# Sort matrices turned by a VectorE block transpose, four more heads expanded on GpSimd, and a newly searched order

## The chip, the cores and the metric

One core of a Trainium2 chip. The time is the device time of one execution in microseconds (us); a kernel's time is the median of its executions. The profile's span is shorter than that time by 1.7 to 2.8 us and is used only for readings inside a run. Engines: TensorE (PE, with its weight loads PEld), VectorE (DVE), ScalarE (ACT), GpSimd (POOL), and SP, which issues the transfers.

A run is called slow when it lies over 1.5 % above the fastest of its kernel, and fast otherwise; the granted TensorE clock is read beside it. Every ratio below is the mean time of one kernel's fast runs over that of the other's in the same rounds, with a 95 % interval, so it is not quite the ratio of the medians that stand next to it.

## The reference, cut to what matters

```python
for _ in range(5):                          # sort_net [4, 8, 8, 8]: 32 (batch, head) pairs
    P = exp(P - max(P, -1)); P /= sum(P, -1) + 1e-9; P /= sum(P, -2) + 1e-9
k_sorted = einsum('bhij,bhjcd->bhicd', P, k_b)      # 8 blocks of 96 rows
v_sorted = einsum('bhij,bhjcd->bhicd', P, v_b)
attn     = softmax(scale * q_b @ k_sorted_b.T)      # inside each block
x        = (attn @ v_sorted_b) as [batch, 768, 512]
val, gate = split(x @ w_in)
h[t]     = exp(A_log)[0] * h[t-1] + val[t]          # scan over 768 steps
out      = (silu(gate) * h) @ w_out
```

## The kernel before

The program lists some 250 operations with dependences; a scheduler inside the kernel sorts them into one list per engine before anything is emitted. Before any block can be sorted, the 32 normalised 8x8 matrices (tile PBF, 32 pairs x 64) have to be turned to 64 x 32, spread over the partitions by TensorE, and multiplied by a mask into block-diagonal weights (tile LALL).

```python
op("ptr_mm", PE,  matmul(PS[u.bank][0:64, 0:NH], PBF, IDENT[0:NH, 0:NH]))
op("ptr_cp", DVE, tensor_copy(PT, PS[u.bank][0:64, 0:NH]))
# pexp_mm: 8 x matmul(..., ESEL[:, i * 128:(i + 1) * 128], PT)
# lmat on VectorE, from PSUM: heads 0-1 (256 columns), heads 2-7 (768 columns)
# pexp_cp: ScalarE copies PSUM to PEXP; lmat on GpSimd, from PEXP: heads 8-31, four at a time
...
for it in range(5):                         # warming matmuls, between the rounds of the normalisation
    for part in range(WARMS[it]):
        op("warm", PE, 4 if it < 4 else 8 matmuls of IDENT by IDENT)
...
P.schedule(8, pull=5.859375, stick=0.1, nudge=NUDGE)
```

Names in the views: L609/L554 transposes of q (line before/line after the change), L625/L570 sorted k and v, L703/L648 scores, L733/L678 attention by values, L662/L607 the other sorted values, L776/L721 transposed activations, L800/L745 input projection, L836/L781 output projection, L754 and L751/L699 and L696 normalisation on VectorE/ScalarE, L713/L658 exponentials. VSS to VA are the moves of sorted values, XN to XT the transposes done by DMA. A q behind an engine's name means its sequencer, which issues; "issue" is time in which an engine waited for nothing that the profile shows.

The softmax here doesn't subtract the row's maximum and nothing guards it: scores larger than these inputs give would overflow.

## Time and profile before

| | before |
|---|---|
| median (range) | 124.22 us (123.44 to 124.76), later rounds 123.8 to 124.7 |
| span of the profiled run, granted clock | 121.7 us, 1.00 |
| TensorE busy, idle | 112.2 us, 9.5 us |
| first expansion on VectorE / first projection | 12.3 / 27.5 us |
| batch 1's moved values landed | 40.3 us |

The table is read from below: the work of TensorE is fixed, so the time is that work plus the time in which TensorE stands still.

### The profile page before, as it was taken

Reading aid. Unit: us, or ns where it says so; the run is one execution under the profiler, and the core shown is the slowest. Engines: PE = TensorE matmul, PEld = TensorE weight load, DVE = VectorE, ACT = ScalarE, POOL = GpSimd, SP = SyncE. Lnnn points to the kernel's source line nnn. Section 1 sums busy time; section 2 is a strip of 40 time slices with the busy share of each in tenths; the row PEclk is TensorE's granted clock in tenths of the full one; section 3 lists DMA queues with packets and bytes.
Section 4 is the critical chain, followed back from the end, with each engine's and each line's share of the span. In section 5 each row is a group of like instructions: output and inputs, shape, how many; then the busy total and the mean of one; then the engine's idle time right before and its main releaser. Section 6 shows DMA issues by size and latency. Waiting matters only on the chain.

```text
span 121.7 us, 3684 instructions
## 1 busy us (share of the span) xinstructions
PE 112.2 (92%) x1485; PEld 74.7 (61%) x1485; DVE 100.0 (82%) x239; ACT 84.0 (69%) x183; POOL 59.5 (49%) x84
## 2 busy tenths in 40 slices
PE   1689989999999999999999999999799999999990
PEld 1577778765766777667556586766466655554530
DVE  3774897999998999977599999999799999995300
ACT  4126879999868988898866977887634423365761
POOL 7999999999955620200028065000011396235500
PEclk9999999999999999999999999999999999999999
DMA  1999999999999999999999868289892000422665
GB/s 6 149 176 188 199 212 209 204 205 203 217 247 236 202 208 215 225 251 239 253 293 251 128 102 154 100 151 144 287 260 48 5 0 0 172 89 86 226 252 216
DMA packets 26305, 21.33 MB, mean 175 GB/s; under 512 B 7472, under 2 KB 22832, under 8 KB 26288
## 3 DMA queue, kind: packets, MB, share of 16 engines
q0 software_dynamic: 13824, 11.01, 58.3%
q1 hardware_dynamic: 12464, 10.08, 30.8%
q8 instruction: 12, 0.20, 0.6%
q14 instruction: 5, 0.04, 0.1%
HBM read 22.03 MB, written 6.29 MB: 233 GB/s over the span
## 4 chain that ended last, share of the span: by engine, by line
PE 66%; DMA 10%; DVE 9%; ACT 4%; SPq 4%; POOL 2%; issue 1%; POOLq 0%
PE PSA L800 31%; PE PSA L836 14%; DMA VA<-VSS 6%; PE PSA L733 5%; DVE XN L754 5%; DMA QB<-in_q_dram 4%; SPq L671 4%; PE PSA L703 4%; PE PSA L609 4%; PE PSA L625 3%; PE PSA L662 2%; ACT EX L713 2%; PE PSA L776 1%; DVE XT L417 1%; DVE RZ L745 1%
## 5 line engine op out<-in xcount | busy, mean ns | idle before, releaser
L819 POOL TENSOR_TENSOR GA<-GA,YS 128x384 bf16<-128x384 bf16 x30 | 27.2, 917 | 55.3 <-DVE GA L816 32.0
L800 PE MATMUL PSA<-XT,WIN 128*128 128x384 bf16 x256 | 45.4, 326 | 0.8 <-DVE XN L754 0.8
L800 PEld LDWEIGHTS PSA<-XT,WIN 128*128 128x128 bf16 x256 | 23.9, 98 | 16.3 <-DVE XN L754 0.9
L713 ACT ACTIVATE EX<-PSA 96x384 bf16<-96x384 f32 x64 | 26.3, 488 | 2.4 <-PE PSA L703 2.1
L813 ACT ACTIVATE TH<-PSA 128x384 f32<-128x384 f32 x32 | 15.7, 492 | 15.0 <-PE PSA L800 13.8
L836 PE MATMUL PSA<-WOUT,GA 128*128 128x512 bf16 (+1 forms) x100 | 23.2, 370 | 0.0
L754 DVE TENSOR_TENSOR XN<-PSA,RZ 96x320 bf16<-96x320 f32 (+2 forms) x49 | 21.7, 470 | 0.2
L816 DVE SCALAR_TENSOR_TENSOR GA<-TH,PSA 128x384 bf16<-128x384 f32 x32 | 17.0, 542 | 5.3 <-ACT TH L813 4.2
L415 ACT ACTIVATE OUTSB<-PSA 128x512 f32<-128x512 f32 (+1 forms) x23 | 13.4, 581 | 7.3 <-PE PSA L836 7.1
L807 DVE TENSOR_TENSOR_SCAN YS<-AEXP,YS,PSA 128x384 bf16<-128x384 f32 x16 | 15.7, 999 | 0.3 <-PE PSA L800 0.2
L807 DVE TENSOR_TENSOR_SCAN YS<-AEXP,PSA 128x384 bf16<-128x384 f32 x16 | 14.8, 940 | 0.7 <-PE PSA L800 0.7
L733 PE MATMUL PSA<-VA,EX 96*128 96x65 bf16 x256 | 13.7, 194 | 0.5 <-DVE XN L754 0.2
L836 PEld LDWEIGHTS PSA<-WOUT,GA 128*128 128x128 bf16 x100 | 9.0, 97 | 8.2 <-ACT OUTSB L415 0.3
L733 PEld LDWEIGHTS PSA<-VA,EX 96*128 96x128 bf16 x256 | 10.9, 98 | 4.7 <-DMA VA<-VSS 0.8
L745 DVE RECIPROCAL RZ<-PSA 96x5 f32<-96x5 f32 (+2 forms) x52 | 8.3, 175 | 2.0 <-PE PSA L733 1.6
L415 ACT ACTIVATE KTS<-PSA 128x768 bf16<-128x768 f32 x11 | 8.6, 811 | 1.4 <-PE PSA L625 1.3
L703 PE MATMUL PSA<-QTS,KTS 64*96 64x96 bf16 x256 | 9.5, 210 | 0.0
L703 PEld LDWEIGHTS PSA<-QTS,KTS 64*96 64x96 bf16 x256 | 7.2, 121 | 3.6 <-DVE KTS L417 0.4
L609 PE MATMUL PSA<-IDENT,QB 128*64 128x128 bf16 x192 | 7.8, 238 | 1.3 <-DMA QB<-in_q_dram 1.3
L415 ACT ACTIVATE VSS<-PSA 128x384 bf16<-128x384 f32 x19 | 8.4, 504 | 0.3 <-PE PSA L662 0.3
L625 PE MATMUL PSA<-LALL,KB 128*64 128x128 bf16 x192 | 7.4, 221 | 0.7 <-ACT EX L713 0.6
L427 POOL DMA_DIRECT2D QB<-in_q_dram x10 | 7.7, 782 | 0.3 <-issue 0.3
(60 smaller groups left out, 122.2 us busy)
## 6 DMA issues: line engine op xcount, KB each, us to landing
out_dram<-OUTSB SPq DMA_DIRECT2D x23, 256.0 KB, 2.5
VA<-VSS SPq DMA_DIRECT2D x24, 97.5 KB, 5.7
VB<-in_v_dram POOLq DMA_DIRECT2D x6, 384.0 KB, 20.1
KB<-in_k_dram POOLq DMA_DIRECT2D x6, 384.0 KB, 23.9
QB<-in_q_dram POOLq DMA_DIRECT2D x6, 384.0 KB, 21.5
WIN<-in_moe_w_in_dram POOLq DMA_DIRECT2D x1, 1024.0 KB, 11.1
QB<-in_q_dram POOLq DMA_DIRECT2D x4, 192.0 KB, 5.1
KB<-in_k_dram POOLq DMA_DIRECT2D x4, 192.0 KB, 6.1
```

What stands on the lines that cost most here:

```text
L415: return eng.activation(dst, src, AF.Copy, scale=1.0 if scale is None else scale)
L609: ins = e.transpose(PSB[u.bank][64 * x:64 * x + 64, t * 128:(t + 1) * 128], QB[sl][:, 2 * pr + x, t * 64:(t + 1) * 64], IDENT[:, :])
L703: ins = e.matmul(PS[us[half, x].bank][0:BLK, il * BLK:(il + 1) * BLK], KTS[ks][r, i * BLK:(i + 1) * BLK], qt(r, i))
L713: op("ex%d_%d_%d" % (p, half, x), act_cost(HALF), lambda e, n, u=us[half, x], es=es, half=half: e.activation(EX[es][:, half, 0:HALF].rearr ...
L733: ins = e.matmul(PS[u.bank][:, (kk - k0) * 65:(kk - k0 + 1) * 65], EX[es][:, i // 4, (i % 4) * BLK:(i % 4) * BLK + 128], VA[vs][:, i, hx * ...
L754: return e.tensor_tensor(XN[xs][:, k0 * D:(k0 + nb) * D].rearrange("p (n d) -> p n d", d=D), pv(u, nb)[:, :, 0:64], bass.AP(RZ[rz], 0, [[6 ...
L800: ins = e.matmul(PS[u.bank][:, 0:HALF], WIN[:, c, col:col + 128], XT[(4 * b + c) % NXT][:, half * HALF:(half + 1) * HALF], start=(c == 0), ...
L807: op("sc%d_%d_%d" % (b, ch, half), {"DVE": 65 + 384 * 2.1}, lambda e, n, u=u: e.tensor_tensor_scan(YS[slot][:, :], AEXP[:, ch:ch + 1].to_b ...
L813: op("th%d_%d_%d" % (b, ch, half), act_cost(HALF), lambda e, n, u=w: e.activation(TH[ts][:, :], PS[u.bank][:, 0:HALF], AF.Tanh, scale=0.5) ...
L816: op("ga%d_%d_%d" % (b, ch, half), dve_cost(HALF), lambda e, n, u=w: e.scalar_tensor_tensor(GA[slot][:, :], TH[ts][:, :], 1.0, PS[u.bank][ ...
L819: op("um%d_%d_%d" % (b, ch, half), {"POOL": 900, "DVE": 500} if b == B - 1 and half else {"POOL": 900}, lambda e, n: e.tensor_tensor(GA[sl ...
L836: ins = e.matmul(PS[u.bank][:, 0:c1 - c0], GA[slots[ch]][:, tl * 128:(tl + 1) * 128], WOUT[:, ch, c0:c1], start=(ch == 0), stop=(ch == 3))
```

## The change

The intent: take a matmul, a copy and two handovers out of the way of the first expansion, relieve VectorE of two thirds of its second expansion, and replay an order that was searched against a new model of the transfers.

```diff
-        op("ptr_mm", {"PE": 120}, lambda e, n, u=up: e.matmul(
-            PS[u.bank][0:64, 0:NH], PBF[:, :], IDENT[0:NH, 0:NH]),
-        op("ptr_cp", dve_cost(32), lambda e, n, u=up: e.tensor_copy(PT[:, :], PS[u.bank][0:64, 0:NH]),
+        op("ptr", dve_cost(64), lambda e, n: e.transpose(PT[:, :], PBF[:, :]), reads=["PBF"], writes=["PT"], prio=-100)
-            for i in range(8):
+            for i in range(4):
-        PT = sb("PT", [64, NH], BF16)
-        ESEL = sb("ESEL", [64, 1024], BF16)
+        PT = sb("PT", [32, 64], BF16)
+        ESEL = sb("ESEL", [32, 512], BF16)
-        for g0, g1 in ((0, 2), (2, 8)):            # VectorE
+        for g0, g1 in ((0, 2), (2, 4)):
-        for g0 in range(8, NH, 4):                 # GpSimd
+        for g0 in range(4, NH, 4):
-        P.schedule(8, pull=5.859375, stick=0.1, nudge=NUDGE)
+        P.replay(8, ORDER)      # five literal lists, one for each engine
...
```

Cut: the five lists themselves, and replay, which takes the order as given and assigns PSUM banks.

## The prediction

> **What bounds the kernel now.** I read the page's busy shares first, then the chain that ended last, then the stretch table, then the timeline of the first 28 us. The page gives TensorE as the engine to watch and the granted clock as full throughout:
>
> ```profile
> PE 112.2 (92%) x1485; PEld 74.7 (61%) x1485; DVE 100.0 (82%) x239; ACT 84.0 (69%) x183; POOL 59.5 (49%) x84
> PEclk9999999999999999999999999999999999999999
> PE 66%; DMA 10%; DVE 9%; ACT 4%; SPq 4%; POOL 2%; issue 1%; POOLq 0%
> ```
>
> The third line is the chain by engine: two thirds of it is TensorE. Busy shares average over stages, so I cut the span (columns: stretch, its length, busy time and count of each engine):
>
> ```profile
> 12.15:26.33 14.18, 13.03 (x287) 10.36 (x285) 12.80 (x37) 12.82 (x28) 14.15 (x27) 1.00 1.24 205
> 26.33:85.31 58.98, 58.76 (x900) 39.17 (x901) 53.99 (x122) 49.07 (x113) 21.50 (x25) 1.00 1.10 201
> 85.31:86.37 1.06, 0.30 (x10) 0.20 (x7) 1.03 (x4) 1.06 (x4) 0.00 (x0) 1.00 0.60 221
> 86.37:118.60 32.23, 32.19 (x204) 18.23 (x204) 25.00 (x43) 15.64 (x31) 12.59 (x14) 1.00 0.40 126
> ```
>
> From 26.3 to 118.6 us TensorE stands still for about 1.3 us in all: 1.06 us at 85.3 and 0.22 us for the moved values at 62. That is where most of the time is, and no step of the expansion of the sort matrices is in it. The change can act on what lies before: the normalisation of the sort matrices (a VectorE and ScalarE chain to 10.9 us), the expansion, and the ramp to 26 us. The chain of waits there:
>
> ```profile
> 8.99 1.49 PE PSA L609 x24
> 10.48 0.97 PE PSA L539 x12
> 11.46 0.14 PE PSA L545
> 11.60 0.03 issue
> 11.62 0.19 DVE PT L548
> 11.81 0.05 issue
> 11.86 0.36 PE PSA L554 x8
> 12.22 0.47 PE PSA L609 x12
> 12.70 0.02 issue
> 12.72 0.81 ACT QTS L415
> 13.53 0.70 ACT KTS L415
> ```
>
> L545 and L548 are the matmul and copy to be removed. The sort matrices are ready at 10.68 + 0.21 = 10.89, but the matmul starts at 11.38, behind warming matmuls, which in turn stood behind transposes of q that came with a late load. Then ScalarE is the chain until 17.6: it copies a last q tile (loaded seventh) before the first sorted k.
>
> **What the skill says.** "VectorE: DVE Perf Modes", section "The three transpose paths": VectorE transposes 32×32 blocks only, into SBUF, 311 ns for sixteen of them. Here there are two blocks, and no such instruction in this trace; my estimate is the time of its small neighbours, 0.2 us (L529, same 32x64 shape: 211 ns). "TensorEngine Tiling (Array Packing)", section "Key Properties": a change of tiling mode drains TensorE. The trace agrees: 24 matmuls of L625 take 0.67 us behind L609 of the same tiling and 0.79 behind L800, so an entry costs about 0.12 us. "SBUF — State Buffer", section "Who interferes with whom": a VectorE instruction with two SBUF inputs contends with a GpSimd instruction that reads SBUF. The expansions on GpSimd took 1.11 to 1.20 us each; VectorE's ramp work reads mostly PSUM, so I add nothing for it.
>
> **The change, part by part.**
> Removed: the 32-column matmul, the 0.18 us copy and two handovers. Now PBF ends at 10.89 and the expansion begins at 11.86, so 0.97 us; with a transpose of 0.2 us and two handovers of 0.04 to 0.06 it would be about 0.3. Gross gain 0.65 us. The expansion has four matmuls in place of eight: 0.36 us less 4 x 0.027 = 0.25. Gain 0.1.
> Added ahead of it: in the new VectorE order the identity (0.23 us) stands inside the first round of the normalisation and the mask (0.38 us) ahead of the fifth round, where VectorE waits only 0.28 us for ScalarE. Before, both lay in idle time. Cost about 0.25 + 0.13 = 0.38 us, so PBF ends near 11.27. Net: the first expansion on VectorE starts at 11.27 + 0.3 + 0.3 = 11.87 against 12.26, a gain of 0.4 us.
> Loads: two q loads now stand ahead of the iota on GpSimd, so the first load leaves some 0.5 us earlier (1.35 to 0.85), and all four q loads come first. No q tile is left to copy after the expansion: first sorted k copy at 12.8 against 13.43 or so, 0.6 us.
> Heads 4 to 7: VectorE's second expansion shrinks from 768 to 256 columns, 0.958 to 0.425 us, so 0.53 us off VectorE in the ramp. GpSimd gets one more of 1.16 us. I place it by adding the GpSimd queue: after fourteen loads it ends near 15 us; the values of heads 4 to 7 then have their weights before the 16.6 us at which they are used now. The weights wait on a path ScalarE, GpSimd, TensorE, but not long enough to show.
> The new order: I decoded the five lists against the operations' numbers. TensorE loses one operation of 251; entries into another tiling go from 55 to 56, 16 of them in the ramp both times. So the work of TensorE is unchanged to 0.2 us, and the order can gain only by closing gaps. In the ramp, six normalisations move to ScalarE (0.87 us each for four activations: L751, 8 in 1.74 us) and copies of k and of transposed outputs move to VectorE.
>
> How large are the gaps? Ramp work from counts in 12.15 to 26.33 and from the closest spacing seen in long runs: 56 x 31 ns (L733), 64 x 22.5 (L703), 32 x 62.5 (L647), 108 x 28 (L625, L609), 20 x 43 (L776), 4 x 163 (L662) = 9.7 us; 16 entries of 0.12 make 11.6. The ramp took 14.18 us, so it holds 2.6 us of slack. Of that, only one wait is named:
>
> ```profile
> PE PSA L625 <- ACT EX L713: 0.6, 1, 0.6
> PE PSA L800 <- DVE XN L754: 0.8, 1, 0.8
> PE PSA L733 <- DMA VA<-VSS: 0.2, 1, 0.2
> ```
>
> The rest hides inside stretched matmuls, which keep TensorE "busy". The ceiling is 0.4 (start) + 2.6 + 1.3 = 4.3 us. How much comes? Adding the new VectorE order with today's durations (copies 0.91 and 0.65, normalisations 0.36, reciprocals 0.15, the half copies 0.3), the copy that releases the first projection ends near 26.2 against 27.2 now. But five sorted-value matmuls (0.8 us) then still follow, which TensorE has done by now in the old order. Net in the ramp 0.6 to 1.2 us; I take 1.0, the start included. For the two later gaps I count 0.3 of the 1.3: the wait at 85.3 stands before the first projection of batch 2, which needs the transposes by DMA of heads 8 to 11 pairs. The new order leaves some 4.75 us of TensorE work between the last of those attention products and that projection, the old one some 4.9, so the wait should mostly come back. Tail: the same last tile, ScalarE copy and store; 0. Sum 1.0 + 0.3 = 1.3 us.
>
> **The rivals.**
> A: the start counts in full and nothing else. TensorE is the bound afterwards, so 0.4 us: 123.8. For it: 92% TensorE. Against: the slack in the ramp is real.
> B: the new order also closes most of the ramp's slack and both later gaps. For it: it was searched with loads and moves modelled anew, as the diff shows (transfers now queue behind each other), so it should fit the transfers better. Gain 2.5 to 3.5 us: 121. Against: VectorE and ScalarE are 90% busy in that ramp (12.80 and 12.82 of 14.18), so they bind with TensorE, and the new order puts slower normalisations on ScalarE.
> C: a new wait takes the place of the old. The values of batch 1 are released later (their last sorted-value matmul follows four projections: I place it near 29.8 against 27.3), and eight moves on the SP queue take 5.2 us to issue and a median 5.7 to land, so the values are there near 42; the new order first reads them near 43. One microsecond of margin. Also, seven DMA transposes and the stores share one queue in order. If both miss, 1 to 2 us are lost and the result is 124 to 125.
> D: the GpSimd expansion of heads 4 to 7 is late (GpSimd is full to 28 us: 14.15 of 14.18) and holds the third and fourth pairs of the values. A slip of 1 us would cost at most that in the ramp: 123.5 to 124.
>
> **Range and chances.** The base median is 124.22 with single runs from 123.44 to 124.76. Minus 1.3 gives 122.9; I lean slightly to B because the order was searched, and say 122.7. A and D lie at 123.5 to 124, B at 121, C at 124 to 125. Eight in ten: 121.3 to 124.2. Faster by over 2% needs under 121.74, a gain of 2.48 of the 4.3 that there is: 0.2. Slower by over 2% needs 2.5 us of new waits on an unchanged amount of work: 0.02. The rest, 0.78, is within 2%.
>
> **What would show it.** Start: the first expansion on VectorE at 11.9 (12.26 now), a transpose of about 0.2 us, PBF near 11.3 in place of 10.9; if PBF is still at 10.9, identity and mask were free and I gave away 0.4. Ramp: TensorE's first projection near 26.3 and its unbroken run from there. Heads 4 to 7: a GpSimd expansion ending by 15 us, and no TensorE wait on it. Later: waits of TensorE on the moved values near 43 and before the first projection of batch 2. Wrong if the gain is mainly after 28 us (I say TensorE's work there is fixed at about 91 us), if entries cost less in the new order, or if a DMA wait over 1 us appears.

## The result, and the profile after

The changed kernel ran in 128.31 us (127.32 to 129.27, four runs) beside 123.85 for the kernel before: ratio 1.032, interval 1.022 to 1.042. It is slower by 3 %, and the prediction of 122.7, range 121.3 to 124.2, missed. The profiled run of the changed kernel: span 125.2 us against 121.7.

The same three lines of the page as the prediction shows of the kernel before, now after the change (busy shares; the clock in tenths; the chain by engine):

```profile
PE 111.7 (89%) x1471; PEld 74.7 (60%) x1480; DVE 99.5 (79%) x234; ACT 85.3 (68%) x196; POOL 61.0 (49%) x86
PEclk9999999958999999999999999999999999999999
PE 57%; ACT 12%; DVE 11%; DMA 10%; SPq 4%; issue 3%; ACTq 0%
```

TensorE's busy time is the same within half a microsecond (and some of its records are missing), so the change is in what it waits for: 125.2 - 111.7 = 13.5 us idle against 9.5. ScalarE's part in the chain has grown from 4 to 12 %, and two digits of the clock are not full. Where the idle time lies shows in busy time by stretch (columns: stretch, length, busy time and count on PE, PEld, DVE, ACT, POOL, then clock, DMA share, GB/s). Before:

```profile
12.00:34.00 22.00, 20.85 (x412) 15.89 (x409) 20.18 (x52) 19.84 (x50) 21.97 (x36) 1.00 1.26 208
34.00:50.00 16.00, 16.00 (x247) 10.74 (x244) 15.31 (x36) 13.36 (x29) 5.67 (x7) 1.00 1.28 223
...
86.00:104.00 18.00, 17.63 (x125) 10.74 (x126) 17.17 (x31) 7.53 (x15) 7.16 (x8) 1.00 0.36 97
```

After:

```profile
12.00:34.00 22.00, 19.55 (x326) 14.82 (x328) 17.00 (x47) 18.96 (x58) 14.16 (x22) 0.92 1.27 205
34.00:50.00 16.00, 14.54 (x218) 9.45 (x216) 13.83 (x24) 12.22 (x27) 14.01 (x18) 1.00 1.19 199
...
86.00:104.00 18.00, 16.98 (x159) 10.79 (x159) 16.17 (x35) 7.03 (x17) 2.93 (x4) 1.00 0.52 131
```

Length less busy time is the idle time: 1.15 became 2.45 us, 0 became 1.46, 0.37 became 1.02. Those are 3.4 us in three places; the two stretches left out differ by under 0.15 us, and most of the rest lies before 12 us (4.28 became 5.01). In the ramp (12 to 34 us) TensorE also got through fewer operations (326 against 412, not all of the same kinds). TensorE's waits of the changed kernel (engine, line, releaser, total, times, longest) name them:

```profile
PE PSA L678 <- DMA VA<-VSS: 1.4, 1, 1.4
PE PSA L570 <- issue: 0.8, 1, 0.8
PE PSA L721 <- ACT XN L696: 0.7, 1, 0.7
...
PE PSA L745 <- ACT EX L658: 0.6, 1, 0.6
...
PE PSA L678 <- ACT EX L658: 0.4, 1, 0.4
```

The first is the wait at 46 us for batch 1's moved values, which land at 47.2 instead of 40.3. The second is a stop at 17 us inside a burst of sorted k, with nothing to wait for. The fourth is at 89 us: the exponential named had ended half a microsecond before, and a transpose by DMA landed just before TensorE went on. The third and fifth are in the ramp, where the chain that ended last runs through ScalarE (start, length, what):

```profile
20.01 0.76 ACT EX L658 x2
20.77 0.80 ACT XN L696 x4
21.57 0.75 ACT EX L658 x2
22.33 1.61 ACT XN L696 x8
23.94 0.38 ACT EX L658
24.32 0.81 ACT XN L696 x4
```

Here normalisations that the new order gave to ScalarE stand between exponentials that TensorE needs. TensorE starves, and then its clock falls; whether the one makes the other is not shown (the same columns as above, one microsecond a line):

```profile
23.00:24.00 1.00, 0.26 (x5) 0.11 (x4) 0.79 (x3) 1.00 (x6) 1.00 (x2) 1.00 1.28 204
24.00:25.00 1.00, 0.93 (x24) 0.80 (x24) 0.55 (x3) 1.00 (x6) 0.32 (x1) 1.00 1.29 199
25.00:26.00 1.00, 0.61 (x16) 0.49 (x11) 0.84 (x4) 1.00 (x6) 0.00 (x0) 0.82 1.33 207
26.00:27.00 1.00, 1.00 (x11) 0.60 (x9) 0.90 (x5) 1.00 (x6) 0.00 (x0) 0.50 1.28 208
```

The clock stays at half until 29 us, and what looks busy there is work at half speed. The first projection starts at 28.7 us, against 27.5 before, although the first expansion starts 0.5 us earlier.

### The profile page after: what moved, and what is told of

Its sections match the earlier page's. It is cut to its first block, busy times and chain, and to the rows that moved or that the text cites.

```text
span 125.2 us, 3660 instructions
## 1 busy us (share of the span) xinstructions
PE 111.7 (89%) x1471; PEld 74.7 (60%) x1480; DVE 99.5 (79%) x234; ACT 85.3 (68%) x196; POOL 61.0 (49%) x86
## 4 chain that ended last, share of the span: by engine, by line
PE 57%; ACT 12%; DVE 11%; DMA 10%; SPq 4%; issue 3%; ACTq 0%
PE PSA L745 21%; PE PSA L781 16%; DMA VA<-VSS 7%; PE PSA L678 5%; ACT EX L658 5%; PE PSA L648 4%; PE PSA L570 4%; SPq L616 4%; DMA XT<-XN 3%; PE PSA L607 3%; ACT XN L696 3%; PE PSA L721 2%; DVE XN L699 2%; PE PSA L554 2%; DVE YS L752 1%
## 5 line engine op out<-in xcount | busy, mean ns | idle before, releaser
L764 POOL TENSOR_TENSOR GA<-GA,YS 128x384 bf16<-128x384 bf16 x31 | 28.0, 921 | 56.8 <-DVE GA L761 45.4
L745 PE MATMUL PSA<-XT,WIN 128*128 128x384 bf16 x256 | 46.9, 327 | 0.9 <-ACT EX L658 0.6
L658 ACT ACTIVATE EX<-PSA 96x384 bf16<-96x384 f32 x64 | 27.0, 496 | 2.8 <-PE PSA L648 2.8
L781 PE MATMUL PSA<-WOUT,GA 128*128 128x512 bf16 (+1 forms) x91 | 21.9, 369 | 0.7 <-ACT EX L658 0.2
L699 DVE TENSOR_TENSOR XN<-PSA,RZ 96x320 bf16<-96x320 f32 (+2 forms) x46 | 21.2, 479 | 1.0 <-DMA XT<-XN 0.5
L364 ACT ACTIVATE OUTSB<-PSA 128x512 f32<-128x512 f32 (+1 forms) x21 | 12.0, 579 | 4.0 <-PE PSA L781 3.9
L364 ACT ACTIVATE KTS<-PSA 128x768 bf16<-128x768 f32 x10 | 7.9, 811 | 0.8 <-PE PSA L570 0.6
L364 ACT ACTIVATE QTS<-PSA 128x768 bf16<-128x768 bf16 x10 | 7.7, 815 | 0.9 <-PE PSA L554 0.8
L488 PE MATMUL PSA<-IDENT 128*128 128x128 bf16 x48 | 4.6, 274 | 4.0 <-DVE CS L476 4.0
## 6 DMA issues: line engine op xcount, KB each, us to landing
KB<-in_k_dram POOLq DMA_DIRECT2D x6, 384.0 KB, 13.5
```

The lines of the kernel that those rows point to most:

```text
L364: return eng.activation(dst, src, AF.Copy, scale=1.0 if scale is None else scale)
L658: op("ex%d_%d_%d" % (p, half, x), act_cost(HALF), lambda e, n, u=us[half, x], es=es, half=half: e.activation(EX[es][:, half, 0:HALF].rearr ...
L699: return e.tensor_tensor(XN[xs][:, k0 * D:(k0 + nb) * D].rearrange("p (n d) -> p n d", d=D), pv(u, nb)[:, :, 0:64], bass.AP(RZ[rz], 0, [[6 ...
L745: ins = e.matmul(PS[u.bank][:, 0:HALF], WIN[:, c, col:col + 128], XT[(4 * b + c) % NXT][:, half * HALF:(half + 1) * HALF], start=(c == 0), ...
L764: op("um%d_%d_%d" % (b, ch, half), {"POOL": 900, "DVE": 500} if b == B - 1 and half else {"POOL": 900}, lambda e, n: e.tensor_tensor(GA[sl ...
L781: ins = e.matmul(PS[u.bank][:, 0:c1 - c0], GA[slots[ch]][:, tl * 128:(tl + 1) * 128], WOUT[:, ch, c0:c1], start=(ch == 0), stop=(ch == 3))
```

## The experiments

Seventeen kernels ran, all with correct results. "Parts" are the block transpose, the halved expansion and the GpSimd expansion of heads 4 to 7; "order" is the five lists. A kernel with one and not the other replays a literal order list in either case.

| kernel | median us | ratio to before (95 %) |
|---|---|---|
| new parts, old order | 125.94 | 1.0147 (1.0098 to 1.0195) |
| old parts, new order | 128.67 | 1.0263 (1.0169 to 1.0356) |
| old order to 33 us, then new | 126.98 | 1.0246 (1.0178 to 1.0315) |
| new order to 33 us, then old | 132.68 | none, mostly slow runs |
| parts, old order, 15 fillers | 123.93 | 0.9999 (0.9974 to 1.0025) |
| changed kernel, 52 fillers | 129.21 | 1.0369 (1.0252 to 1.0487) |
| changed, normalisations on VectorE | 127.06 | 1.0257 (1.0179 to 1.0334) |
| changed, weights loaded early | 128.05 | 1.0329 (1.0287 to 1.0372) |
| changed, both of these and 52 fillers | 128.2 | 1.0244 (1.0175 to 1.0314) |
| parts, old order, 15 fillers, later start | 123.53 | 0.9952 (0.9927 to 0.9977) |
| old order to 50 us, then new | 128.3 | 1.0315 (1.0208 to 1.0421) |
| new order to 80 us, then old | 128.24 | 1.0238 (1.0119 to 1.0357) |
| changed, last third repaired | 127.34 | 1.0146 (1.0023 to 1.0269) |
| changed, three repairs | 126.12 | 1.0140 (1.0039 to 1.0241) |
| before, 5 warming matmuls fewer | 125.23 | 0.9999 (0.9959 to 1.0039) |
| parts, old order, 5 fillers | 123.92 | 0.9983 (0.9954 to 1.0012) |
| parts, old order, 5 fillers, later start | 124.00 | 0.9979 (0.9949 to 1.0010) |

### Parts against order

```diff
 parts only:  new ptr, pexp, lmat    ORDER = what the old scheduler decided
 order only:  old ptr_mm, ptr_cp, pexp, lmat    ORDER = the new lists
```

> The changed instructions (VectorE transpose, four expansion matmuls, heads 4 to 7 expanded on GpSimd) under the old order of every engine. Theory O (the order does the harm): 123.0 to 123.8 us, 0 to 0.8 under the kernel before, the first expansion on VectorE near 11.5 us because identity and mask stand where they did, first projection at 27.5 or earlier, no drop of the granted clock. Rival P (the parts do the harm, heads 4 to 7 wait for GpSimd): over 125 us, a TensorE wait before the values of heads 4 to 7.

> The old instructions (transpose by matmul and copy, heads 2 to 7 on VectorE) under the new order. Theory O: 127.5 to 129 us like the changed kernel, with the clock drop between 25 and 29 us and the ramp late by 2 us or more. Rival P: 123.5 to 125 us.

Neither is faster. The order alone (1.026) costs most of the 3.2 %. The parts alone, which should gain, cost 1.5 %, some 1.8 us: the number of the rival, but not its reason, since no wait on the GpSimd expansion shows. The waits of the parts-only run hold a line that the kernel before has not:

```profile
PE PSA L570 <- issue: 1.2, 1, 1.2
```

Loads came late in that run too (TensorE waited 3.2 us for q in all), and the first projection came at 29.2 us, so the stop need not be all of the loss. TensorE stopped at 57.9 us between two matmuls of sorted k that depend on nothing new. Counting TensorE's instructions in the traces (two to a matmul with its weight load, one to a semaphore instruction) puts this stop at number 1,728 and the stop at 17 us in the changed kernel at 448: both are 448 + 256 k. A transfer of 16 KB in the queue named "instruction" starts 2.3 to 2.4 us before TensorE goes on, in either case. So the theory: instructions come in blocks of 256, and a stop shows where the end of a block falls into matmuls of some 28 ns.

### Which half of the new order

```diff
 first kernel:   old order for what is scheduled by about 33 us, new order for the rest
 second kernel:  new order for what is scheduled by about 33 us, old order for the rest
```

> Changed kernel, but all that comes before and with the last sorted-value matmul of batch 1 in the old order; the rest in the new order. Theory R (the loss is made in the ramp, and the wait of 1.4 us for the moved values follows from it): 123 to 125 us, no clock drop, wait for moved values under 0.5 us. Rival L (the later order does it by itself): 126 to 128.

> The other half: ramp in the new order, the rest in the old. Theory R: 126 to 128.5 us, clock drop near 25 us again. Rival L: 123.5 to 125 us.

With the old ramp 2.5 % stay, rival L's figure. The wait for moved values is gone there and the clock is full (0.998 or more in four runs), as theory R expected, but at 45 us TensorE waits 1.6 us for a product of the gates on GpSimd. With the new ramp the kernel is worst, but its profiled run and two more are slow ones with a clock near 0.96, so only the direction is used: both halves cost, as far as cuts can show it, for the place where two orders meet can make waits of its own.

### The place of the fetch

The parts make TensorE's stream ten instructions shorter (five matmuls; three semaphore instructions more make it seven by the end). Extra warming matmuls shift the block ends back.

```diff
-                    for i in range(4 if it < 4 else 8):          # in the old order with the new parts
+                    for i in range((9 if part == 0 and it == 0 else 4) if it < 4 else 8):
```

> The new parts in the old order once more, with five matmuls more in the first warm-up operation, so that TensorE's stream is again as many instructions long as before the change. Theory F (an instruction fetch, which comes once per 256 TensorE instructions, fell into the burst of short matmuls of the sorted keys at 57.9 us and stopped TensorE there for 1.2 us, because the change shortened the stream by ten instructions): the wait of 1.2 us named 'issue' before the sorted keys goes, and the kernel is 1.0 to 1.4 us faster than the same kernel without the five, 124.4 to 125.0. Theory L (the loads of that run came late and cost the time, the fetch is noise): no change, 125.5 to 126.5, and the wait comes back there or near.

0.9999, 1.5 % better than without filling. But the edit was wrong: the loop variable was read after its loop, so that 15 matmuls were added, five to each of three operations. The next run has the same fault: 52 fillers instead of 44.

> The changed kernel with 44 more warm-up matmuls, spread over the warm-up operations in time that TensorE spends waiting before the expansion, so that the first 256-instruction boundary falls before the bursts of sorted values and keys at 15.9 to 16.9 us instead of inside the last. Theory F: the stop of 0.8 us at 17 us goes, and if nothing else takes it the kernel gains 0.4 to 0.8 us, 127.4 to 127.9. Theory A (what bounds the ramp is ScalarE with its expansions and normalisations, and TensorE only waits for it): under 0.2 us, 128.1 to 128.5, though the stop goes.

No gain: 129.21 lies above both ranges, and the profiled run is a slow one. The stop at 17 us is gone, but the premise that TensorE merely waits there was wrong: the chain shows 68 warming matmuls in a row for 6.60 us, 97 ns each, and the first expansion came at 14.5 us instead of 11.7. The start came 2.8 us later and the ratio moved by only 0.5 %, inside the intervals: a first hint at what the start is worth.

With the fault mended (the variable bound in the definition), five fillers in one operation, and, as a counter-check, five matmuls fewer in the kernel before, which has nothing of the change in it:

```diff
+                    for i in range((9 if part == 0 and it == 0 else 4) if it < 4 else 8):   # parts, old order
+                    for i in range(((1, 2, 4)[part] if it == 0 else 4) if it < 4 else 8):   # the kernel before
```

> The new parts in the old order with truly five warm-up matmuls more in one operation. (The earlier run of that description emitted fifteen, five in each of the first three operations, by a mistake in the edit; its stream was 20 instructions longer than before's, not equal.) Theory F: as many instructions as before, the boundary at the place of before: 0.996 to 1.003 of before. Rival L: 1.010 to 1.020, like the new parts without filling.

> The kernel before the change, with nothing of the change in it, but five warm-up matmuls fewer, so that its TensorE stream is ten instructions shorter, as with the new parts. Theory F (the position of the 256-instruction fetch in the burst of sorted keys makes the 1.2 us that the new parts lost): a stop of 0.8 to 1.4 us shows at 55 to 57 us and the kernel is slower by 0.6 to 1.5 us, 1.005 to 1.012 of before. Rival L (late loads of one run and the new parts themselves made that loss): 0.998 to 1.003 of before, no stop over 0.4 us.

Five matmuls take the parts from 1.0147 to 0.9983, and no "issue" wait is left. In the kernel before, five fewer bring the stop, at the same number 1,728:

```profile
PE PSA L625 <- issue: 1.1, 1, 1.1
```

That the stop follows the count and not the parts is shown. The count alone does not suffice: in the run with the weights loaded early (below) the 448th instruction is the same one as in the changed kernel, its transfer started at 14.3 us instead of 15.3, and no stop shows. The price of the stop in the kernel before is not shown: the median of all 20 runs is 125.23 against 124.46, the ratio of the fast runs 0.9999, because eleven of the twenty, all at a clock of 0.996 or more, lie over 1.5 % above the fastest and are left out as slow.

### Is the earlier start worth anything

```diff
-        op("ptr", ..., lambda e, n: e.transpose(PT[:, :], PBF[:, :]), ...)
+        op("ptr", ..., lambda e, n: [e.transpose(PT[:, 64 * x:64 * x + 64], PBF[:, :]) for x in range(3)][-1], ...)
         # PT [32, 192], of which the last third is used
```

> The new parts in the old order with the five matmuls of filling, and two more transposes of 0.23 us on VectorE ahead of the one that counts, so that the sort matrices start about 0.45 us later, where they started before the change. Theory B (the start is covered: what the first expansion gains is waited for again at the loads of keys, which land one a microsecond until 17.7 us in either kernel): 0.9990 to 1.0020 of before, as without the delay. Rival G (the start is on the path, and something else in the new parts ate its gain): 0.4 us slower than without the delay, 1.003 to 1.005 of before.

> The new parts in the old order, five warm-up matmuls more, and two more transposes ahead of the one that counts, so that the first expansion starts about 0.45 us later. With fifteen fillers the later start measured 0.9952 of before against 0.9999 with the early one. If a later start is a gain by itself, 0.993 to 0.997; if the early start is merely worth nothing (theory B), 0.997 to 1.001, as with five fillers and no delay (0.9983); if it is worth its 0.45 us (rival G), 1.001 to 1.003.

The first pair (15 fillers) even favours the later start by 0.5 %, which I cannot explain. The second pair (five fillers) is the cleaner one: 0.9983 early, 0.9979 late. The first expansion on VectorE (line, count, duration, first and last start) and TensorE's wait for q in the profiled runs; early start, then late:

```profile
L505 DVE TENSOR_TENSOR LALL<-PSA,MASK x2: 425/425/425, 11.6 to 12.1; 128x256 bf16<-128x256 f32 x2
PE PSA L554 <- DMA QB<-in_q_dram: 2.3, 3, 1.2
```

```profile
L505 DVE TENSOR_TENSOR LALL<-PSA,MASK x2: 424/424/425, 12.9 to 13.3; 128x256 bf16<-128x256 f32 x2
PE PSA L554 <- DMA QB<-in_q_dram: 1.4, 2, 1.0
```

In these two runs the start moved by 1.3 us and the span by 0.1 (122.0 and 121.9); the wait for loads took up 0.9 us of it. The edit itself is the smaller part: three transposes in a row took 0.49 us instead of 0.23 for one. The rest is TensorE, whose transposes of q and warming matmuls ahead of the expansion took longer in the second run (24 of q 1.49 us instead of 0.86). A delay of 0.26 us alone is less than the intervals can tell, so the reading rests on this pair of profiled runs. The loads set the ramp: 192 KB each at the 208 GB/s of that stretch is 0.95 us a load, and the last of the twelve that batch 0 needs lands at 17.6 us both before and after the change.

### Repairs of the new order, one wait at a time

```diff
 normalisations:  six operations of the ramp from ScalarE's list back to VectorE's, each behind its reciprocal
 weights:         the load of w_out on GpSimd's list moved ahead of heads 16-19's expansion, behind the last q load of batch 1
 both:            these two and the 52 fillers
```

> The changed kernel with the six normalisations of the ramp that the new order gave to ScalarE put back on VectorE, each behind the reciprocal it needs; all else as changed. Theory A (ScalarE, busy without a break from 18.5 to 28 us, is what holds TensorE in the ramp; TensorE idles at 23.2 and 25.2 us, its granted clock then falls to half from 26 to 29 us): the two waits for normalisations and exponentials go, the clock stays at 1.00, the first projection comes at 27.3 to 28.0 instead of 28.8, and the time is 126.3 to 127.5. Rival V (VectorE, 0.79 busy in the ramp, cannot take six more of 0.55 us; the wait moves to VectorE's normalisations): the first projection at 28.5 or later and the time 128.0 to 129.0. Rival T (the ramp does not set the end; the moves of the sorted values do, landing at 47.3): the ramp gains, the wait at 46 us grows by as much, and the time stays within 0.4 of 128.3.

> The changed kernel with one load moved: the 1 MB of the output weights, which the new order issues at 36.3 us among the moves of batch 1's sorted values (issued 33.7 to 39.0, landed 47.3), is issued some ten microseconds earlier, behind the last query load, so that it stands ahead of the moves in the queue. Theory M (the 1.4 us that TensorE waits at 46 us are bandwidth: load and moves share it): the moves land 1.5 to 2.5 us earlier, at 45 to 46, the wait is under 0.3 us, and the kernel gains 0.8 to 1.4, 126.9 to 127.5. Rival S (the moves are late because the sorted values are, and waiting for them covers other lateness that then shows, such as transposed activations at 89 us): the wait goes, the time changes less than 0.4 from 128.3.

> The changed kernel with three repairs at once: the six ramp normalisations on VectorE, the load of the output weights early, and 44 more warm-up matmuls so that no fetch falls into the sorted keys at 17 us. Theory A+M+F (the three waits make up the difference, 1.2 measured for the first, 1.0 to 1.4 and 0.4 to 0.8 expected for the others): 124.4 to 125.4, within 1.2 % of before. Rival S (the new order loses as much again in the half after 50 us, where its transposes of activations land late): 126.0 to 127.0, no better than with the first repair alone by more than 0.6.

The normalisations gave 1.0257 for 1.0322, the size expected (1.3 us by the medians), but the intervals overlap; the first projection came at 28.2 us instead of 28.7, later than expected; the clock stayed at 0.997 or more in three of four runs; in the changed kernel's four it was 0.971 to 0.984. The early weights took the wait for moved values away and gained nothing. TensorE's waits of that run, and its stretches:

```profile
PE PSA L745 <- DMA XT<-XN: 2.3, 2, 1.6
```

```profile
34.00:50.00 16.00, 15.94 (x238) 10.24 (x238) 14.97 (x28) 13.63 (x31) 13.73 (x17) 1.00 1.27 220
...
86.00:104.00 18.00, 15.54 (x146) 9.88 (x146) 15.52 (x34) 6.34 (x14) 2.53 (x3) 1.00 0.42 126
```

Idle time from 34 to 50 us fell from 1.46 to 0.06; from 86 to 104 us it rose from 1.02 to 2.46. TensorE came earlier to projections whose inputs, transposed by DMA, did not. The third kernel was spoiled by its fillers: its first expansion came at 14.4 us.

### Cuts at 50 and at 80 us

> The new parts, in the old order up to about 50 us and in the new order from there to the end; the cut is closed under the dependences and under each engine's order. With the cut at 33 us it was 126.98 (1.0246 of before). Theory M (the new order loses its second part between 33 and 50 us, where loads, moves of sorted values and GpSimd's gating come late): 124.2 to 125.4, under 1.012 of before. Rival T (it loses it in the last third, where the transposed activations land late and the projections of batch 2 wait at 88 to 100 us): 126.3 to 127.5, no better than the cut at 33.

> The mirror image: the new parts in the new order up to about 80 us and in the old order from there to the end. The whole new order ran in 128.05 to 128.3. Theory M (all that the new order loses is lost by 50 us, and the waits for activations at 88 to 100 us only show it again): 127.7 to 128.8, no change. Rival T (the tail of the new order costs 1.0 to 1.5 us by itself): 126.6 to 127.3, and no wait for transposed activations over 0.3 us after 85 us.

At 50 us both theories missed. At 80 us the median lies in the range of theory M, but two of the four runs are slow, and the fast ones (127.08 and 127.44) lie near that of theory T. With the old order up to 50 us TensorE is nearly as little idle there as before (1.61 and 0.05 us in the first two stretches), yet the new rest loses it all, at a clock of 0.999 or more in all four runs, so a loss of this size needs no fall of the clock:

```profile
50.00:70.00 20.00, 18.36 (x261) 11.16 (x258) 13.16 (x26) 14.60 (x30) 2.04 (x3) 1.00 0.99 185
...
86.00:104.00 18.00, 16.60 (x157) 10.38 (x156) 16.01 (x35) 7.31 (x17) 2.40 (x3) 1.00 0.58 133
```

With the new order up to 80 us and the old tail, TensorE is idle for 1.18 us from 86 to 104 us, 1.1 of it one wait for transposed activations. As each cut can make waits of its own, these two do not divide the loss; that it does not lie in one part is read from the stretches above, not shown by the cuts.

### All repairs without fillers

```diff
 tail, SP:       - store 3, transpose 9, store 5, transposes 11, 10, stores 8, 10, 7, transpose 14, stores 11, 6, transposes 13, 12
                 + store 3, transposes 9, 11, 10, store 5, transpose 12, stores 8, 10, 7, transpose 14, stores 11, 6, transpose 13
 tail, VectorE:  pair 13's last reciprocal and normalisation ahead of its second
 three repairs:  tail + normalisations + weights
```

> The changed kernel with two repairs in its last third alone: three transposed activations are started ahead of a store and of a transposition that is not ready, and the last normalisation of pair 13 goes ahead of those of pairs 14 and 15 on VectorE. Theory R (each wait of the new order is its own loss): TensorE's idle time between 86 and 104 us falls from 1.0 to under 0.4 and the time by 0.5 to 0.8, to 127.4 to 127.8. Rival S (what is not waited for there is waited for elsewhere): idle time in the whole run stays within 0.4 us of 13.5, the time within 0.4 of 128.3.

> The changed kernel with the three repairs that lengthen nothing: the six ramp normalisations on VectorE, the load of the output weights early, and the repairs of the last third. No warm-up matmuls are added, since those of the earlier triple repair turned out to hold the first expansion back by 2.7 us. Theory R: TensorE's idle time goes from 13.5 to between 10.5 and 11.5 us, and the time to 125.0 to 126.0. Rival S: idle time 12.5 or more, the time 126.5 to 127.5.

The tail alone gave 1.0146 from two fast runs, more than expected; its profiled run is a slow one and still waits 1.3 us for transposed activations, so how it gained is not shown. The three together: 1.0140, and the profiled run (124.8 us, fast) is idle for 11.9 us. TensorE's waits in it:

```profile
PE PSA L570 <- DMA KB<-in_k_dram: 0.8, 2, 0.6
PE PSA L745 <- DMA XT<-XN: 0.6, 1, 0.6
PE PSA L721 <- DVE XN L699: 0.5, 2, 0.3
```

The result lies between what the two theories expected, nearer to "each wait its own loss": 1.8 of the 3.2 per cent came back. That this took all three is not shown, as the tail alone measured as much from two fast runs. And in this run the clock fell to half again, from 25.7 to 29.1 us, although the six normalisations are back on VectorE.

## Why the prediction was wrong, step by step

**Start: right in size, wrong in worth.** The first expansion was predicted at 11.87 and came at 11.7 us; the block transpose took 0.23 us (estimate 0.2); identity and mask cost 0.2 us instead of 0.38. But the step that adds this gain to the end failed. In the pair of profiled runs with early and late start 1.3 us there changed the span by 0.1: the loads cover them. The first load left 0.1 us earlier (1.25 against 1.35), not the 0.5 that the step on loads counted.

**Parts: a term was missing.** No step looked at the length of TensorE's instruction stream. In the old order the parts cost 1.5 % until five matmuls of filling took it back; the stop that shows is 1.2 of these 1.8 us, and the counter-check shows the stop without a price. In the changed kernel the stop falls at 17 us, 0.8 us; what it costs there is open.

**Ramp: the term of 1.0 us gained in the ramp has the wrong sign.** I noted that six normalisations of about 0.87 us move to ScalarE and that ScalarE was busy 12.82 of 14.18 us, and then laid out only VectorE's new order to date the first projection. It came at 28.7, not 26.3. ScalarE is the chain, TensorE starves behind it and runs at half clock for about 3 us. With the six back on VectorE the profiled run kept its clock, but that of the three repairs did not (first projection at 28.2 and 28.4 us): ScalarE's place in the chain is shown by the trace, why the clock falls is not.

**Gaps: "an unchanged amount of work" was right, "the order can gain only by closing gaps" was half of it.** It can also open gaps, and opened 3.4 us. The step gave a chance of 0.02 to 2.5 us of new waits. A reading was off too: of the 1.06 us at 85.3 TensorE was busy for 0.30, so the ceiling of 4.3 us was 0.3 too high.

**Rival C was the mechanism in two of the three places.** I placed the moved values at 42, read at 43. They were issued from 33.6 to 38.8, later than I placed them (28.5 to 33.2 before), and the last took 8.4 us to land, not the median 5.7, as the 1 MB of weights was under way among them. With that load early, the wait goes. C gave 1 to 2 us for the moved values and the transposes by DMA; idle time grew there by 1.46 and 0.65. Its sum, 124 to 125, left out the ramp, whose idle time grew by 1.3 us, and a second wait behind the first; the run with the early weights shows one.

**Heads 4 to 7: right.** The GpSimd expansion was done at 14.2 us, and no wait for it shows in TensorE's list.

**Open.** The three repairs leave 1.4 %. I did not find one cause for it: the clock is still 0.986 in the profiled run, and 2.4 us of idle time are spread. Why the searched order expected less is not tested either. No version beats the kernel before by 2 %; the best, parts in the old order with 15 fillers and the later start, measured 0.9952.

## What to carry to other kernels

Before counting an earlier start as gain, ask what the next stage waits for: delay the start on purpose, and if nothing moves, it is covered. When an order changes, add up each engine's chain in the tightest stage, above all the engine that receives work, and look for the next wait behind each one that you repair. A change of a few instructions on TensorE can move an instruction fetch into a burst of short matmuls; a few filling matmuls tell that apart from a real loss.

## What the Trainium skill lacked or had wrong

- "Runtime: NRT & Kernel Launch", section "Instruction fetch mechanics": blocks of 256 instructions are confirmed (stops at 448 + 256 k, transfers of 16 KB). That crossing a block is "mostly hidden" failed at these places: TensorE stopped for 0.8 to 1.2 us in bursts of matmuls of about 28 ns. Lacking: in the traces of the kernel before, of the changed one, of the parts alone and of the two kernels with five matmuls more or fewer, the fetch began 1.3 to 5.3 us after TensorE passed the last block end while loads ran (to about 68 us), and at most 1.6 us after it from there to 100 us; that the loads delay it is a guess, no run tests it.
- "TensorE: Matmul & The Clock Gate", section "What's actually happening": two clock values only, and about 3.4 us of half speed, agree (0.50 from 25.6 to 29 us). It ties the fall to an idle window of about 3.4 us; a later section of the page names frequent short gaps too, without a figure. Here no idle stretch over 0.74 us lay in the 4 us before the fall, only three microseconds with TensorE 0.26, 0.93 and 0.61 busy; with the three repairs it fell after 0.68, 0.97 and 0.87, and with the normalisations alone it stayed full after 0.68, 0.99 and 0.98.
- No page that I read has the time of transposes by DMA beside other transfers: 2.9 to 4.5 us to landing before the change, up to 5.6 with the weights loaded early.
